# Long-convolution mixer and two feed-forward layers on one core: one unsplit block of eight instead of two, more splitting on POOL, and a 40-byte gap between POOL's operands

## The chip, the cores and the metric

The kernel runs on one core of a Trainium2 chip. The metric is the device time in microseconds of one execution; of several executions the median counts. Lower is better.

## What is computed

The reference, cut to its core (float32 throughout):

```
u = x * v                                    # x, v: 2 x 12480 x 128
h = (max(pos_emb @ w1, 0) @ w2) * exp(-0.01 * pos)
y = irfft(rfft(u, 2S) * rfft(h, 2S))[:S]     # long convolution along the sequence
a = x * y                                    # 24960 tokens x 128
h1 = a @ w_in1                               # 128 -> 2048
g1 = where(h1 > 0, h1, exp(min(h1, 0)) - 1)
b = g1 @ w_out1                              # 2048 -> 128
h2 = b @ w_in2
out = (h2 * cos(h2)) @ w_out2
```

## The kernel before

The work runs in three stages on one core, each engine with its own queue in program order. The order is written out by hand (`tc.manual_schedule()`), and the tile framework only adds the semaphores.

**Filter taps and convolution** (to about 690 us). The convolution is done as matrix products with DFT tables (`st_a` to `st_d`), and beside it the four weight matrices, which arrive as 64-bit floats, are decoded to float32, split in two and written to DRAM (`Decode`, from L109). POOL takes part with element-wise products, sums and differences.

**Layer 0 and layer 1** (from about 690 us to the end). Tokens stand in 52 tiles of T = 480 columns for each layer; the 2048 hidden features of a tile are done in NBLK = 8 blocks m of 256 (two halves e of 128). The loop at the end of the kernel (L641 to L656) goes through 2 x 52 x 8 = 832 blocks n. In iteration n it issues, in this order: `gemm1(n)`, at one block of the tile `split_x` for the next tile, in layer 1 `cosine(n - 1)`, the splits `split_g` of blocks one and two iterations old, and `gemm2(n - 5)` (LAG = 5).

A float32 product is done in one of two ways. **Split:** each factor is taken apart into a high part that TensorE reads in its reduced float32 (F32R) and a remainder, and three products are added: high x high, low weight x high, high weight x low. `gemm1` (L545) always does this: per block 2 halves x 3 = 6 matmuls of 480 columns. `gemm2` (L614) does it in blocks that are marked split: 6 matmuls. **Whole:** in a block marked `F.` in PLAN, `gemm2` multiplies unsplit float32 (tile `gf`, weights `wf`): one product per half, which stands as two matmul instructions in the trace, so four a block.

```
PLAN = ("AP PP F. AP PP F. PP PP".split(), "AP PP F. AP PP F. PP PP".split())
```

PLAN names for each layer and block who splits the activation g into `gh` and `gl` (`halves`, L102 to L107): the first letter is the engine of the rounding copy `gh` (A: ACT, L98, an ACTIVATE; P: POOL, L106, a TENSOR_SCALAR), the second that of the difference `gl = g - gh` (P: POOL, L107, a TENSOR_TENSOR of two inputs). Both are 128 x 960. A whole block gives POOL nothing to do. In layer 0 a block `PP` is split one iteration after its gemm1 and a block `AP` two after (`DELAY`, `DELAY_A`), the `PP` one first where both fall in one iteration; in layer 1 all are split two after. The state x of the next tile is split on POOL too (`xh`, `xl`, 128 x 480, `split_x` L525), issued at block 4 of a tile.

Activations: layer 0 takes Exp and Tanh on ACT (L556, L558) and two passes on DVE (L560, L562); layer 1 takes a rounding copy and Sin on ACT (L573, L582) and two passes on DVE (L575, L584). The activation g lies in the tile `e2` (shown as `e`), of which there are EB = 4 buffers; `gh` and `gl` have 5 each.

`skewed(pool, ...)` (L91) makes a tile 16 elements longer and starts the data `by` elements into it. SKEWS gives such starts for e2, gh and gl by layer and block, from 0 to 16 elements of 4 bytes:

```
SKEWS = (((0, 2, 0), (0, 10, 0), (0, 0, 0), (0, 4, 0), (0, 8, 0), (0, 0, 0), (0, 1, 0), (0, 10, 10)),
         ((2, 2, 0), (0, 0, 2), (0, 0, 0), (0, 6, 0), (0, 14, 0), (0, 0, 0), (2, 0, 2), (0, 16, 0)))
```

So in layer 0 `gh` of block 1 begins 40 bytes past a plain start while `e2` and `gl` begin at one; in layer 1 `e2` and `gh` of block 0 both begin 8 bytes past one. In the state split `x_in` and `xh` both begin at a plain start.

Weights are loaded whole for a layer: layer 0's on ACT's queue before its first block, layer 1's on SP's queue (`reload`) during the last tile of layer 0. A split block of output weights is 256 KB in two parts, a whole block 128 KB from `wf_d`, which `Decode.parts` writes in addition.

Of the kernel before, what the change touches and what calls it, by code (L numbers as in the profile page):

```python
# [9 lines left out]
F32 = mybir.dt.float32  # L10
F32R = mybir.dt.float32r
# [7 lines left out]
B, S, D, FO, DFF = 2, 12480, 128, 64, 2048  # L19
NA = 98  # L20
# [9 lines left out]
T = 480  # L30
NTC = B * S // T
NFT = DFF // 128
NBLK = NFT // 2
LAG = 5


PLAN = ("AP PP F. AP PP F. PP PP".split(), "AP PP F. AP PP F. PP PP".split())
FULL = [[m for m in range(NBLK) if p[m] == "F."] for p in PLAN]
XSPLIT = "PP"
EB = 4  # L40


SKEW = 10
SKEWS = (((0, 2, 0), (0, 10, 0), (0, 0, 0), (0, 4, 0), (0, 8, 0), (0, 0, 0), (0, 1, 0), (0, 10, 10)),
         ((2, 2, 0), (0, 0, 2), (0, 0, 0), (0, 6, 0), (0, 14, 0), (0, 0, 0), (2, 0, 2), (0, 16, 0)))

DELAY = (1, 2)
DELAY_A = (2, 2)
# [33 lines left out]
def hyena_moe_kernel(ctx: ExitStack, tc: tile.TileContext, x, v, pe, w1, w2,  # L82
# [8 lines left out]
    def skewed(pool, shape, dt, by, **kw):  # L91

        n = int(np.prod(shape[1:]))
        t = pool.tile([shape[0], n + 16], dt, **kw)[:, by:by + n]
        return t if len(shape) == 2 else t.rearrange("p (a b) -> p a b", a=shape[1])
# [6 lines left out]
    def halves(plan, hi, lo, full):  # L102
        if plan[0] == "A":
            copy_r(hi, full)
        else:
            ENG[plan[0]].tensor_scalar(hi, full, 1.0, 0.0, op0=ALU.mult, op1=ALU.add)  # L106
        ENG[plan[1]].tensor_tensor(lo, full, hi.bitcast(F32), op=ALU.subtract)  # L107
# [67 lines left out]
    with tc.manual_schedule():  # L175
        nc.vector.memset(below, BELOW)
        with ExitStack() as cs:
# [26 lines left out]
            with ExitStack() as fs:  # L204
                fp = fs.enter_context(tc.tile_pool(name="fp", bufs=4))
                f1 = fs.enter_context(tc.tile_pool(name="f1", bufs=1))
                f3 = fs.enter_context(tc.tile_pool(name="f3", bufs=3))
# [3 lines left out]
                NP = 4  # L211
# [13 lines left out]
                pes, rs, rr, hp_ = {}, {}, {}, {}  # L225
# [36 lines left out]

                def relu(c):
                    r = f3.tile([2 * FO, NP * NA], F32, name="r")
                    r_h = f3.tile([2 * FO, NP * NA], F32R, name="r_h")
                    r_l = f3.tile([2 * FO, NP * NA], F32R, name="r_l")
                    nc.scalar.activation(r, rs.pop(c), AF.Relu)
                    nc.gpsimd.tensor_scalar(r_h, r, 1.0, 0.0, op0=ALU.mult, op1=ALU.add)
                    nc.gpsimd.tensor_tensor(r_l, r, r_h.bitcast(F32), op=ALU.subtract)
                    rr[c] = (r_h, r_l)  # L270
# [40 lines left out]
            with ExitStack() as vs:  # L311
                p1 = vs.enter_context(tc.tile_pool(name="p1", bufs=1))
                p2 = vs.enter_context(tc.tile_pool(name="p2", bufs=2))
# [116 lines left out]
                    nc.sync.dma_start(xt_d[k, c * DC:(c + 1) * DC].rearrange("d a b -> a d b"), at)  # L430

                def alloc(name, dt):
                    return (p1 if name in ("sq", "keep", "power", "size") else p2).tile([128, 256], dt, name=name, tag=f"d_{name}")

                jobs = [(l, w, q) for l in range(2) for w in range(2) for q in range(DFF // 256)]
                ready = []
# [1 line left out]
                def bits_of_all():  # L438
                    nxt = Decode(alloc, 256, *jobs[0])
                    for i in range(len(jobs)):  # L440
                        dec = nxt
                        if i + 1 < len(jobs):
                            nxt = Decode(alloc, 256, *jobs[i + 1])
                        yield from dec.bits()
                        ready.append(dec)
# [33 lines left out]
        xp = ctx.enter_context(tc.tile_pool(name="xp", bufs=2))  # L479
        ep = ctx.enter_context(tc.tile_pool(name="ep", bufs=2))  # L480
        gp = ctx.enter_context(tc.tile_pool(name="gp", bufs=LAG))
# [37 lines left out]
        def load_x(j, q=nc.sync):  # L519
            if j < NTC:  # L520
                b, o = divmod(j * T, S)
                xin[j] = xp.tile([128, T], F32, name="x_in", tag="io")
                q.dma_start(xin[j], xt_d[b].rearrange("d a b -> d (a b)")[:, o:o + T])

        def split_x(l, j):  # L525
            src = xin.pop(j) if l == 0 else x1[:, j * T:(j + 1) * T]
            xh = xp.tile([128, T], F32R, name="xh")
            xl = xp.tile([128, T], F32R, name="xl")
            halves(XSPLIT, xh, xl, src)
            xsp[l, j] = (xh, xl)  # L530

        def g_tile(l, m, t):
            if m in FULL[l]:
                return skewed(gp, [128, 2, T], F32, 0, name="gf", tag="gh")
            return t

        def gemm1(n):
            l, j, m = blocks[n]
            xh, xl = xsp[l, j]

            def product(h, e):
                f = 2 * m + e
                wh, wl = layers[l].wt(0, 0, f), layers[l].wt(0, 1, f)
                for k, (a, b) in enumerate(((wh, xh), (wl, xh), (wh, xl))):
                    nc.tensor.matmul(h[:, 0:T], a, b, start=k == 0, stop=k == 2)  # L545

            if l == 0:
                hp, tp = hp_pool[0]
                u = skewed(ep, [128, 2, T], F32, SKEWS[l][m][0], name="e2", bufs=EB)
                gt = g_tile(l, m, u)  # L550
                hs, ts = [], []
                for e in range(2):
                    hs.append(hp.tile([128, 512], F32, name="h_ps"))
                    product(hs[e], e)
                for e in range(2):
                    nc.scalar.activation(u[:, e], hs[e][:, 0:T], AF.Exp)  # L556
                    ts.append(tp.tile([128, 512], F32, name="t_ps"))
                    nc.scalar.activation(ts[e][:, 0:T], hs[e][:, 0:T], AF.Tanh, scale=0.5)  # L558
                for e in range(2):
                    nc.vector.scalar_tensor_tensor(u[:, e], u[:, e], 1.0, ts[e][:, 0:T], op0=ALU.add, op1=ALU.mult)  # L560
                for e in range(2):
                    nc.vector.scalar_tensor_tensor(gt[:, e], u[:, e], 0.0, hs[e][:, 0:T], op0=ALU.min, op1=ALU.max)  # L562
                pend[n] = gt
            else:
                if 1 not in hp_pool:
                    ps0.close()
                    hp_pool[1] = ctx.enter_context(tc.tile_pool(name="hp2", bufs=3, space=PSUM))
                h = hp_pool[1].tile([128, 2, 512], F32, name="h_ps2")
                for e in range(2):
                    product(h[:, e], e)  # L570
                hv = h[:, :, 0:T]
                kq = ep.tile([128, 2, T], I32, name="e1")
                nc.scalar.activation(kq, hv, AF.Copy, scale=1.0 / TWO_PI, bias=0.25)  # L573
                rr = skewed(ep, [128, 2, T], F32, SKEWS[l][m][0], name="e2", bufs=EB)
                nc.vector.scalar_tensor_tensor(rr, kq, -TWO_PI, hv, op0=ALU.mult, op1=ALU.add)  # L575
                mid[n] = (rr, hv)

        def cosine(n):
            if n not in mid:
                return  # L580
            rr, hv = mid.pop(n)
            nc.scalar.activation(rr, rr, AF.Sin, bias=half_pi)  # L582
            gt = g_tile(*blocks[n][::2], rr)
            nc.vector.tensor_tensor(gt, rr, hv, op=ALU.mult)  # L584
            pend[n] = gt

        def split_g(n):
            if n not in pend:
                return
            gt = pend.pop(n)  # L590
            l, j, m = blocks[n]
            if m in FULL[l]:
                gg[n] = (gt, None)
                return
            gh = skewed(gp, [128, 2, T], F32R, SKEWS[l][m][1], name="gh")
            gl = skewed(gp, [128, 2, T], F32R, SKEWS[l][m][2], name="gl")
            halves(PLAN[l][m], gh, gl, gt)
            gg[n] = (gh, gl)

# [25 lines left out]
        def reload(n, wh):  # L625
            l, j, m = blocks[n]
            if l == 0 and j == NTC - 1:
                layers[1].load(nc.sync, wh, m)
# [8 lines left out]
        def delay(n):  # L637
            l, _, m = blocks[n]
            return (DELAY_A if PLAN[l][m][0] == "A" else DELAY)[l]

        for n in range(NBK + LAG):  # L641
            if n < NBK:
                l, j, m = blocks[n]
                gemm1(n)
                reload(n, 0)
                if m == NBLK // 2:
                    nl, nj = (l, j + 1) if j + 1 < NTC else (l + 1, 0)
                    if nl < 2:
                        split_x(nl, nj)
                    if l == 0:  # L650
                        load_x(j + 2)
            cosine(n - 1)
            for d in range(1, LAG):
                if 0 <= n - d < NBK and delay(n - d) == d:
                    split_g(n - d)
            if n >= LAG:  # L656
                gemm2(n - LAG)
                reload(n - LAG, 1)
# [38 lines left out]
```

## Time and profile before

| what | value |
|---|---|
| median of 3 runs | 2953.85 us (2953.04 to 2956.12) |
| the profiled execution | 2956.76 us, of it the span 2955.0 us |
| PE (matmul) busy | 2927.4 us, 99% of the span |
| DVE busy | 2507.0 us, 85% |
| POOL busy | 2426.0 us, 82% |
| ACT busy | 2074.1 us, 70% |
| mean granted TensorE clock | 0.994 of full speed |
| matmuls | 13268 |

The span runs from the first to the last instruction; the 1.76 us above it lie around it. Busy shares are means over the stages. Matmuls overlap and their ends are modelled, so PE's cost is better read from the distance between the starts of its groups in the timeline than from the busy time. A number in brackets behind an instruction of the timeline is the idle time of its engine just before it, and what ended it.

### The profile page before, as it was taken

What the parts mean: (1) busy time and instruction counts of PE and PEld (TensorE: products, weight loads), DVE (VectorE), ACT (ScalarE), POOL (GpSimd) and SP (SyncE); (2) the same over time, 40 slices, a digit from 0 to 9 for tenths busy, and PEclk for the clock granted to TensorE, in tenths of its full rate; (3) what the DMA queues carried; (4) which work ended last, traced back from release to release, by engine and by line L of the source; (5) the groups of instructions that cost most, each with busy time, mean ns of one, the idle gap of its engine ahead of it and who ended that gap; (6) DMA issues with size and microseconds to landing.
All of it is one profiled execution on the core that took longest, in us unless ns stands there. A gap on an engine that the chain in (4) does not pass through costs nothing.

```text
span 2955.0 us, 38859 instructions
## 1 busy us (share of the span) xinstructions
PE 2927.4 (99%) x13268; PEld 2340.5 (79%) x13268; DVE 2507.0 (85%) x3241; ACT 2074.1 (70%) x3228; POOL 2426.0 (82%) x1700
## 2 busy tenths in 40 slices
PE   8999999998999999999999999999999999999999
PEld 6878788786888887888888887887888888888887
DVE  5888888887888888888888888888888888888887
ACT  3323222324888888888888887888888888888887
POOL 5888888885888888888888887888888888888887
PEclk9999999998999999999999999999999999999999
DMA  3333333323000000000000001000000000000000
GB/s 104 89 84 92 89 95 90 86 75 93 11 11 14 11 14 11 14 11 11 14 11 14 11 11 54 11 14 10 14 11 11 14 11 14 11 14 11 12 13 14
DMA packets 82583, 96.19 MB, mean 33 GB/s; under 512 B 6107, under 2 KB 67577, under 8 KB 82387
## 3 DMA queue, kind: packets, MB, share of 16 engines
q1 hardware_dynamic: 76960, 88.07, 10.4%
q10 hardware_dynamic: 5426, 5.65, 0.6%
q8 instruction: 106, 1.74, 0.2%
q14 instruction: 91, 0.74, 0.1%
HBM read 59.16 MB, written 34.54 MB: 32 GB/s over the span
## 4 chain that ended last, share of the span: by engine, by line
PE 98%; DVE 1%; ACT 0%; issue 0%; POOL 0%; DMA 0%; POOLq 0%; ACTq 0%; DVEq 0%
PE o_ps L614 39%; PE h_ps L545 37%; PE ps_b L377 7%; PE ps_c L409 6%; PE ps_a L341 4%; PE ps_d L427 4%; PE h_ps L278 1%; PE w_ps L219 0%; PE r_ps L260 0%; DMA xt_d<-at 0%; ACT t_ps L558 0%; ACT e L556 0%; DVE e L562 0%; POOLq L693 0%; POOL u_t L322 0%
## 5 line engine op out<-in xcount | busy, mean ns | idle before, releaser
L107 POOL TENSOR_TENSOR gl<-e,gh 128x960 fp32r<-128x960 f32 x624 | 1272.8, 2047 | 147.7 <-ACT gh L98 113.0
L545 PE MATMUL h_ps<-xh,w 128*128 128x480 f32 x3328 | 1073.6, 403 | 10.4 <-DVE e L562 7.9
L545 PEld LDWEIGHTS h_ps<-xh,w 128*128 128x128 f32 x3328 | 627.6, 189 | 190.0 <-issue 85.5
L614 PE MATMUL o_ps<-gh,w 128*128 128x480 f32 x2496 | 748.1, 381 | 0.0
L575 DVE SCALAR_TENSOR_TENSOR e<-e,h_ps 128x960 f32<-128x960 int32 x416 | 480.2, 1154 | 199.7 <-ACT e L573 144.8
L560 DVE SCALAR_TENSOR_TENSOR e<-e,t_ps 128x480 f32<-128x480 f32 x832 | 542.8, 653 | 121.8 <-ACT t_ps L558 109.5
L545 PE MATMUL h_ps<-xl,w 128*128 128x480 f32 x1664 | 632.7, 380 | 0.1
L106 POOL TENSOR_SCALAR gh<-e 128x960 fp32r<-128x960 f32 x416 | 415.8, 1000 | 233.8 <-DVE e L562 174.1
L556 ACT ACTIVATE e<-h_ps 128x480 f32<-128x480 f32 x832 | 472.8, 568 | 186.5 <-PE h_ps L545 131.9
L573 ACT ACTIVATE e<-h_ps 128x960 int32<-128x960 f32 x416 | 404.5, 972 | 197.1 <-PE h_ps L545 194.1
L614 PEld LDWEIGHTS o_ps<-gh,w 128*128 128x128 f32 x2496 | 469.4, 188 | 76.0 <-issue 0.8
L614 PE MATMUL o_ps<-gl,w 128*128 128x480 f32 x1248 | 475.1, 381 | 1.9 <-POOL gl L107 1.9
L558 ACT ACTIVATE t_ps<-h_ps 128x480 f32<-128x480 f32 x832 | 475.8, 572 | 0.0
L582 ACT ACTIVATE e<-e,half_pi 128x960 f32<-128x960 f32 x416 | 453.4, 1090 | 0.3 <-DVE e L575 0.3
L562 DVE SCALAR_TENSOR_TENSOR e<-e,h_ps 128x480 f32<-128x480 f32 x624 | 377.9, 647 | 0.0
L614 PE MATMUL o_ps<-gf,wf 128*128 128x480 f32 x832 | 368.5, 565 | 0.0
L584 DVE TENSOR_TENSOR e<-e,h_ps 128x960 f32<-128x960 f32 x312 | 357.9, 1147 | 1.3 <-ACT e L582 1.2
L545 PEld LDWEIGHTS h_ps<-xl,w 128*128 128x128 f32 x1664 | 313.1, 188 | 50.9 <-POOL xl L107 0.8
L614 PEld LDWEIGHTS o_ps<-gl,w 128*128 128x128 f32 x1248 | 235.0, 188 | 40.1 <-POOL gl L107 2.7
L614 PEld LDWEIGHTS o_ps<-gf,wf 128*128 128x128 f32 x832 | 156.9, 189 | 100.8 <-issue 88.7
L98 ACT ACTIVATE gh<-e 128x960 fp32r<-128x960 f32 x208 | 208.2, 1001 | 11.0 <-PE o_ps L614 11.0
L377 PE MATMUL ps_b<-z_t,dft_t 128*128 128x360 f32 x512 | 165.7, 466 | 1.9 <-DVE y_t L393 1.7
(90 smaller groups left out, 3458.7 us busy)
## 6 DMA issues: line engine op xcount, KB each, us to landing
x_t<-in_x SPq DMA_DIRECT2D x32, 392.0 KB
v_t<-in_v SPq DMA_DIRECT2D x32, 392.0 KB
xt_d<-at SPq DMA_DIRECT2D x64, 196.0 KB
out<-ot SPq DMA_DIRECT2D x52, 240.0 KB
x_in<-xt_d SPq DMA_DIRECT2D x50, 240.0 KB
raw<-in_wi SPq DMA_DIRECT2D x16, 256.0 KB
w_d<-hi SPq DMA_DIRECT2D x32, 128.0 KB
w_d<-lo SPq DMA_DIRECT2D x32, 128.0 KB
```

Of the source, the lines that this page charges most:

```text
L106: ENG[plan[0]].tensor_scalar(hi, full, 1.0, 0.0, op0=ALU.mult, op1=ALU.add)
L107: ENG[plan[1]].tensor_tensor(lo, full, hi.bitcast(F32), op=ALU.subtract)
L377: nc.tensor.matmul(ps[:, r, 0:n], a[:, sl], b[:, q], start=j == 0 and i == 0, stop=j == 1 and i == len(mm) - 1)
L545: nc.tensor.matmul(h[:, 0:T], a, b, start=k == 0, stop=k == 2)
L556: nc.scalar.activation(u[:, e], hs[e][:, 0:T], AF.Exp)
L558: nc.scalar.activation(ts[e][:, 0:T], hs[e][:, 0:T], AF.Tanh, scale=0.5)
L560: nc.vector.scalar_tensor_tensor(u[:, e], u[:, e], 1.0, ts[e][:, 0:T], op0=ALU.add, op1=ALU.mult)
L562: nc.vector.scalar_tensor_tensor(gt[:, e], u[:, e], 0.0, hs[e][:, 0:T], op0=ALU.min, op1=ALU.max)
L573: nc.scalar.activation(kq, hv, AF.Copy, scale=1.0 / TWO_PI, bias=0.25)
L575: nc.vector.scalar_tensor_tensor(rr, kq, -TWO_PI, hv, op0=ALU.mult, op1=ALU.add)
L582: nc.scalar.activation(rr, rr, AF.Sin, bias=half_pi)
L614: nc.tensor.matmul(o, a, b[:, e], start=f == 0 and k == 0, stop=f == NFT - 1 and k == len(mm) - 1)
```

## The change

One block of eight (block 3) is whole in both layers, where blocks 2 and 5 were. The block that is now split in addition is split by POOL alone, so POOL makes five `PP` blocks a tile instead of four; two `AP` blocks remain (0 and 4, where 0 and 3 were). The starts of tiles that POOL reads together are set 40 bytes apart everywhere: SKEWS goes, `e2` and `gl` begin at a plain start and `gh` ten elements in; `xh`, the relu's `r_h` and, in the weight decoding, `lf` and `hi` get the same ten elements. In layer 1 the next tile's state is split at block 5 in place of 4; `load_x`, which stands in the same branch, is issued in layer 0 alone, where the block stays 4.

```diff
-PLAN = ("AP PP F. AP PP F. PP PP".split(), "AP PP F. AP PP F. PP PP".split())
+PLAN = ("AP PP PP F. AP PP PP PP".split(), "AP PP PP F. AP PP PP PP".split())
 FULL = [[m for m in range(NBLK) if p[m] == "F."] for p in PLAN]
 XSPLIT = "PP"
+
+XAT = (4, 5)
 EB = 4
 
-
 SKEW = 10
-SKEWS = (((0, 2, 0), (0, 10, 0), (0, 0, 0), (0, 4, 0), (0, 8, 0), (0, 0, 0), (0, 1, 0), (0, 10, 10)),
-         ((2, 2, 0), (0, 0, 2), (0, 0, 0), (0, 6, 0), (0, 14, 0), (0, 0, 0), (2, 0, 2), (0, 16, 0)))
...
-                    r_h = f3.tile([2 * FO, NP * NA], F32R, name="r_h")
+                    r_h = skewed(f3, [2 * FO, NP * NA], F32R, SKEW, name="r_h")
...
-                    return (p1 if name in ("sq", "keep", "power", "size") else p2).tile([128, 256], dt, name=name, tag=f"d_{name}")
+                    pool = p1 if name in ("sq", "keep", "power", "size") else p2
+                    if name in ("lf", "hi"):
+                        return skewed(pool, [128, 256], dt, SKEW, name=name, tag=f"d_{name}")
+                    return pool.tile([128, 256], dt, name=name, tag=f"d_{name}")
...
-            xh = xp.tile([128, T], F32R, name="xh")
+            xh = skewed(xp, [128, T], F32R, SKEW, name="xh")
...
-                u = skewed(ep, [128, 2, T], F32, SKEWS[l][m][0], name="e2", bufs=EB)
+                u = ep.tile([128, 2, T], F32, name="e2", bufs=EB)
...
-                rr = skewed(ep, [128, 2, T], F32, SKEWS[l][m][0], name="e2", bufs=EB)
+                rr = ep.tile([128, 2, T], F32, name="e2", bufs=EB)
...
-            gh = skewed(gp, [128, 2, T], F32R, SKEWS[l][m][1], name="gh")
-            gl = skewed(gp, [128, 2, T], F32R, SKEWS[l][m][2], name="gl")
+            gh = skewed(gp, [128, 2, T], F32R, SKEW, name="gh")
+            gl = gp.tile([128, 2, T], F32R, name="gl")
...
-                if m == NBLK // 2:
+                if m == XAT[l]:
```

## Rows read from the trace of the kernel before

**Rows 1.** The page: busy time of the engines; chain that ended last, by engine.

```profile
PE 2927.4 (99%) x13268; PEld 2340.5 (79%) x13268; DVE 2507.0 (85%) x3241; ACT 2074.1 (70%) x3228; POOL 2426.0 (82%) x1700
...
PE 98%; DVE 1%; ACT 0%; issue 0%; POOL 0%; DMA 0%; POOLq 0%; ACTq 0%; DVEq 0%
```

**Rows 2.** Windows (stretch: us, busy per engine, PEclk, DMA share, GB/s).

```profile
690.00:725.00 35.00, 26.84 (x86) 18.64 (x85) 20.99 (x37) 19.65 (x39) 17.36 (x13) 0.77 0.31 93
...
1000.00:1400.00 400.00, 400.00 (x1709) 321.00 (x1708) 356.50 (x595) 336.00 (x650) 329.11 (x224) 1.00 0.04 12
...
2300.00:2700.00 400.00, 400.00 (x1713) 321.62 (x1712) 330.03 (x299) 331.13 (x355) 338.29 (x224) 1.00 0.03 12
```

**Rows 3.** Timeline of PE, layer 1: start, us, what.

```profile
2203.93 0.60 PE L614 MATMUL o_ps<-gh,w 128*128 128x480 f32 x2
...
2206.56 0.60 PE L614 MATMUL o_ps<-gh,w 128*128 128x480 f32 x2
...
2209.15 1.77 PE L614 MATMUL o_ps<-gf,wf 128*128 128x480 f32 x4
2210.39 0.97 PE L545 MATMUL h_ps<-xh,w 128*128 128x480 f32 x2
...
2212.06 0.60 PE L614 MATMUL o_ps<-gh,w 128*128 128x480 f32 x2
...
2231.87 0.97 PE L545 MATMUL h_ps<-xh,w 128*128 128x480 f32 x2
```

**Rows 4.** Timeline of POOL, one tile of layer 0.

```profile
1016.70 1.00 POOL L106 TENSOR_SCALAR gh<-e 128x960 fp32r<-128x960 f32 x1 [1.38 <-DVE e L562]
1017.78 4.48 POOL L107 TENSOR_TENSOR gl<-e,gh 128x960 fp32r<-128x960 f32 x2
1022.20 1.01 POOL L106 TENSOR_SCALAR gh<-e 128x960 fp32r<-128x960 f32 x1
...
1025.16 1.00 POOL L106 TENSOR_SCALAR gh<-e 128x960 fp32r<-128x960 f32 x1
...
1030.12 0.99 POOL L106 TENSOR_SCALAR gh<-e 128x960 fp32r<-128x960 f32 x1 [1.99 <-DVE e L562]
1031.20 3.74 POOL L107 TENSOR_TENSOR gl<-e,gh 128x960 fp32r<-128x960 f32 x2
...
1038.24 0.99 POOL L106 TENSOR_SCALAR gh<-e 128x960 fp32r<-128x960 f32 x1 [1.43 <-DVE e L562]
```

**Rows 5.** Timeline of POOL, layer 1.

```profile
2220.47 2.28 POOL L107 TENSOR_TENSOR gl<-e,gh 128x960 fp32r<-128x960 f32 x1 [1.32 <-ACT gh L98]
2222.71 1.00 POOL L106 TENSOR_SCALAR gh<-e 128x960 fp32r<-128x960 f32 x1
2223.80 2.28 POOL L107 TENSOR_TENSOR gl<-e,gh 128x960 fp32r<-128x960 f32 x1
2226.04 0.59 POOL L106 TENSOR_SCALAR xh<-x 128x480 fp32r<-128x480 f32 x1
2226.72 1.24 POOL L107 TENSOR_TENSOR xl<-x,xh 128x480 fp32r<-128x480 f32 x1
2228.61 1.89 POOL L107 TENSOR_TENSOR gl<-e,gh 128x960 fp32r<-128x960 f32 x1 [0.65 <-ACT gh L98]
```

**Rows 6.** Groups by line and shape, 120 to 690 us (convolution): busy us, mean ns.

```profile
L322 POOL TENSOR_TENSOR u_t<-x_t,v_t 98x512 f32<-98x512 f32 x56 | 61.2, 1093 | 0.0
```

**Rows 7.** Timeline of all engines, last tile of layer 1.

```profile
2925.63 0.59 PE L545 MATMUL h_ps<-xh,w 128*128 128x480 f32 x2
...
2932.25 1.15 DVE L584 TENSOR_TENSOR gf<-e,h_ps 128x960 f32<-128x960 f32 x1
...
2943.97 1.00 POOL L106 TENSOR_SCALAR gh<-e 128x960 fp32r<-128x960 f32 x1 [0.89 <-DVE e L584]
...
2947.99 2.22 POOL L107 TENSOR_TENSOR gl<-e,gh 128x960 fp32r<-128x960 f32 x1
...
2950.26 0.49 PE L614 MATMUL o_ps<-gl,w 128*128 128x480 f32 x1 [1.60 <-POOL gl L107]
```

## The prediction

> **What bounds the kernel now.** I read the page first: PE is busy 99% of the span and 98% of the chain that ended last is PE's [rows 1]. Its busy time alone would not say that it is full, since the ends of matmuls are modelled; so I looked for gaps. In the windows PE is busy for all 400 us of a stretch of layer 0 and all 400 us of one of layer 1, at a full granted clock (1.00, the 2.4 GHz level), while DVE, ACT and POOL all leave idle time [rows 2]. So in both layers the end is set by what PE has to issue, and a change is worth what it takes off PE, as long as no other engine needs longer than a tile of PE.
>
> Next, what a block costs PE, from the starts of its groups [rows 3]. From one split block's gemm2 to the next (one gemm1 and one gemm2, 12 matmuls of reduced float32) takes 2206.56 - 2203.93 = 2.63 us, and 2.59 us to the next start, at 2209.15. That one is a whole block: its four matmuls delay the following gemm1 to 2210.39, the pass runs on into it, and the next gemm2 begins at 2212.06, 2.91 us after the whole one began. So a whole block is not the cheaper one, although it has four matmuls for six: it costs 0.3 us more. As a check, six blocks of 2.61 and two of 2.91 make 21.48 us, and the two tile starts shown lie 2231.87 - 2210.39 = 21.48 apart. (2209.15 is block 2's gemm2, which stands in the tile's last iteration, so a tile begins right after.) In layer 0 POOL's round takes 1038.24 - 1016.70 = 21.54 us [rows 4].
>
> **The change, part by part. PE:** each tile trades one whole block for one split one. With a tile at 21.53 us and the whole block at 2.91, the split one is (21.53 - 5.82) / 6 = 2.62, the difference 0.29 us; the rows themselves allow 0.28 to 0.32. Over 2 x 52 tiles that is 30.2 us saved (29 to 33). A tile then takes PE 21.24 us.
>
> **POOL** gets the work. Its round in layer 0 [rows 4]: the pair at 1016.70 is blocks 4 and 3 (PP first), then 6 at 1022.20 and 7 at 1025.16, then the pair 1 and 0 of the next tile at 1030.12, after which the state is split. A gl pass takes 4.48 / 2 = 2.24 us in blocks 4 and 3, whose gh starts 32 and 16 bytes past e, but 3.74 / 2 = 1.87 us in blocks 1 and 0 (40 and 8 bytes). In layer 1 it takes 2.28 us where e and gh start alike (blocks 0 and 1) [rows 5], and 2.22 us with 64 bytes between (block 7, in the last tile) [rows 7]. So what the gap of 40 bytes is worth is in the trace: block 1 of layer 0 has just the arrangement that all blocks get. I take 1.87 us for each gl. A PP split then costs 2.96 us from start to start (1022.20 to 1025.16), an AP split 1.87. The state: 0.68 us from xh to xl, and xl goes from 1.24 us [rows 5] to about 1.02, if a product of two inputs that are already 40 bytes apart, 1.093 us for 512 elements [rows 6], is scaled to 480; bounds 1.0 and 1.24.
>
> The sum for a tile: 5 x 2.96 + 2 x 1.87 + 0.68 + 1.02 = 20.24 us, against PE's 21.24. POOL fits, with 1.0 us to spare where layer 0 shows 1.38 + 1.99 = 3.37 us of idling now [rows 4]. It becomes the bound where the seven gl passes take over 1.87 + 1.0 / 7 = 2.01 us each.
>
> A page speaks against the new split here: the Trainium skill, GPSIMD Engine Reference, Performance versus the Vector engine, puts a two-input pass at about 2.6 cycles an element at 1.2 GHz, a floor of its read port; as an estimate from that page 960 elements take 2.08 us, seven passes 1.5 us more than in my sum, and POOL would set the tile at 21.7 us. The trace disagrees where the gap is 40 bytes (1.87 us) [rows 4].
>
> **Is POOL in time as well?** Follow layer 1, with times from a tile's first gemm1 (2210.39 in [rows 3]). Today block 3's gl starts at 2228.61 [rows 5], 18.22 in; the AP block there will be block 4, one iteration later: 20.84. Then gl 4, PP 5, 6 and 7 run without a pause to 20.84 + 1.87 + 3 x 2.96 = 31.6, which is 10.35 of the next tile. Block 0's gl, at 10.08 today, waits 0.3 us, and blocks 1 and 2 and the state follow to 10.35 + 1.87 + 5.92 + 1.70 = 19.84. There POOL idles until 20.84, so the queue closes on itself and doesn't grow. Who waits: the next tile's first product needs the state at 21.24 (it is split last before that, and the move by a block is why: at block 4 it would stand ahead of block 2's split), 1.4 us to spare. Block 7's gl, done at 31.6, is wanted by its gemm2 at 21.24 + 4 x 2.62 + 0.29 + 1.31 = 33.3, so 1.7 us early. In layer 0 the PP blocks go one iteration earlier, so they have 2.62 us more in hand than here; block 7, queued behind PP 5, gl 4 and PP 6, uses up 2.96 + 1.87 + 2.96 - 2 x 2.62 = 2.5 us of it. None of these reaches PE.
>
> **The rest, at nothing each.** The gaps in the relu, the weight decoding and the state make POOL's passes shorter in stages where PE sets the pace; a gain there is worth 0, a loss I can exclude by the same rows. The whole blocks' extra writes fall by 128 KB a layer on SP's queue; loads grow by 128 KB a layer, layer 0's on ACT's queue ahead of the first block: at the 93 GB/s of that stretch [rows 2] at most 1.4 us, if the last load is what the first gemm2 waits for. Layer 1's stand in SP's queue a tile ahead of their use. `load_x` is not moved.
>
> **The end.** In the last tile POOL is late already: PE waits 1.60 us for the last gl [rows 7]. Now block 5 is in that queue too, and POOL's 0.89 us of idling before block 6 goes. The three last splits take 3 x 2.96 and finish no sooner than today; between 0 and +2 us, I take +1.
>
> **Sum:** -30.2 + 1.0 = -29.2 us. The profiled execution took 2956.8 us (span 2955.0 and 1.8 around it), so 2927.6. The median of the runs lies 2.9 us below the profiled one, so about 2925 for a median.
>
> **The rivals.** (a) *POOL sets the end*, the case on the slower side. The shorter pass belongs to today's placements of buffers and doesn't carry over: e2 and gl become 64 bytes shorter. Then gl costs 2.28 us; PP, as block 1 of layer 1 shows, 2226.04 - 2222.71 = 3.33 us, and the tile 5 x 3.33 + 2 x 2.24 + 0.68 + 1.24 = 23.05 us, 1.5 more than now: 2954 + 104 x 1.52 = 3112. It decides from 2.01 us a pass on. Against it: with four buffers of e and five of gh in turn, the passes shown keep to their 1.87 or 2.24 by gap alone. Chance 0.04.
>
> (a') *POOL's pass has a floor somewhere between*, above the 2.01 us at which it decides and below the 2.24 us of the next rows up. At their middle, 2.12, the tile is 20.24 + 7 x 0.25 = 21.99 us and the time 2954 + 104 x 0.46 = 3002. Against it: the passes of [rows 4, 5] with 8, 24 or 40 bytes between e and gh stand at 1.87 to 1.89. Chance 0.02. The skill's page named above would put the pass at 2.08 us and so the time at about 2973, an estimate from that page.
>
> (b) *A second chain, of ACT and DVE, is just as full in layer 1*, and part of the gain is lost. h has three buffers there, so gemm1 of block n + 3 waits for block n's second DVE pass. That pass ended 2933.40 for a gemm1 begun at 2925.63, 7.77 us [rows 7], and three split iterations last 7.86. Today each such slow block (those whose ACT queue carries an AP copy) has a whole gemm2 within those three iterations; block 2 will not, as the whole block's gemm2 moves to iteration 0. If ACT is 0.1 to 0.3 us later, PE waits that long once a tile: 52 x 0.1 to 0.3 = 5 to 15 us back, 2930 to 2940. A late state split would look alike. Chance 0.12.
>
> (c) *No net effect*, 2954: whole and split blocks cost the same in place, or waits eat all of 0.29 us. [Rows 3] speak against it. Chance 0.03.
>
> **How the numbers follow.** The forecast, PE's tile shorter by 0.28 to 0.32 us in both layers, has 0.79: 2925, and with its bounds (29 to 33 us saved, 0 to 2 at the end, up to 1.4 at the loads) 2920 to 2928. Runs of before spread over 3 us, so 2918 to 2931 for it. To hold 8 in 10 with the sizes' own errors I take in (b)'s nearer part, up to 2937. A measurement can tell about 0.2%, 5.9 us: all of the forecast and all of (b) lie beyond that, (a) and (a') are slower and (c) within, apart from a little of (b) that could come out worse.
>
> **What would show it.** Right: starts of two split gemm2 still 2.62 us apart, one 2.91 in a tile, tile starts 21.24 apart; all gl at 1.87 to 1.9, xl near 1.02; POOL busy about 95% of both layers with one pause of some 1 us a tile, before gl of block 4 or PP 5; PE at 100% in the windows. Wrong: gl at 2.2 or more (a); PE gaps of 0.1 to 0.3 us once a tile, released by DVE L584 at block 5's gemm1 (b) or by POOL xl at a tile's start; a split block's 2.62 us grown.

## The result and the profile after

The changed kernel takes 2927.34 us (median of 4 runs, 2926.68 to 2929.37) against 2953.44 for the kernel before: a ratio of 0.991, 95% interval 0.9898 to 0.9923, or 26.1 us less. The forecast was 2925, with 2918 to 2937. The profiled execution took 2926.68 us, of it the span 2924.9.

First the same lines of the page and the windows as in [rows 1, 2].

```profile
PE 2895.9 (99%) x13476; PEld 2377.2 (81%) x13476; DVE 2502.7 (86%) x3241; ACT 2060.4 (70%) x3228; POOL 2587.7 (88%) x1908
...
PE 97%; POOL 1%; DMA 1%; ACT 1%; DVE 1%; issue 0%; ACTq 0%; POOLq 0%; DVEq 0%
```

```profile
1000.00:1400.00 400.00, 400.00 (x1770) 333.09 (x1769) 360.21 (x604) 339.02 (x661) 368.63 (x265) 1.00 0.05 13
...
2300.00:2700.00 400.00, 400.00 (x1770) 332.29 (x1769) 333.89 (x302) 333.39 (x359) 369.12 (x265) 1.00 0.03 12
```

208 matmuls more and yet less time: PE is busy in all 400 us of both stretches, as it was, but more tiles go through them. POOL stands at 368.6 and 369.1 of 400 us, where it had 329.1 and 338.3.

The timeline of PE in layer 1 answers to [rows 3]:

```profile
2206.84 0.59 PE L616 MATMUL o_ps<-gh,w 128*128 128x480 f32 x2
...
2208.15 0.60 PE L547 MATMUL h_ps<-xh,w 128*128 128x480 f32 x2
...
2209.46 1.77 PE L616 MATMUL o_ps<-gf,wf 128*128 128x480 f32 x4
2210.70 0.98 PE L547 MATMUL h_ps<-xh,w 128*128 128x480 f32 x2
...
2212.39 0.60 PE L616 MATMUL o_ps<-gh,w 128*128 128x480 f32 x2
...
2215.01 0.60 PE L616 MATMUL o_ps<-gh,w 128*128 128x480 f32 x2
...
2230.70 1.77 PE L616 MATMUL o_ps<-gf,wf 128*128 128x480 f32 x4
```

A split block still takes 2209.46 - 2206.84 = 2.62 us (and 2215.01 - 2212.39 = 2.62 after the whole one), the whole one 2212.39 - 2209.46 = 2.93, and there is one whole block from tile to tile, 2230.70 - 2209.46 = 21.24 us apart. The six matmuls of a split gemm2 hold PE for 2208.15 - 2206.84 = 1.31 us, 0.22 each. A gemm1 takes another 1.31, so the four of the whole block cost 2.93 - 1.31 = 1.62 us, 0.40 each.

POOL's timeline of one tile of layer 1, from one pause to the next, answers to [rows 5]:

```profile
2207.41 1.88 POOL L106 TENSOR_TENSOR gl<-e,gh 128x960 fp32r<-128x960 f32 x1 [1.05 <-ACT gh L97]
2209.26 0.99 POOL L105 TENSOR_SCALAR gh<-e 128x960 fp32r<-128x960 f32 x1
2210.33 1.88 POOL L106 TENSOR_TENSOR gl<-e,gh 128x960 fp32r<-128x960 f32 x1
2212.18 1.00 POOL L105 TENSOR_SCALAR gh<-e 128x960 fp32r<-128x960 f32 x1
...
2216.20 3.90 POOL L106 TENSOR_TENSOR gl<-e,gh 128x960 fp32r<-128x960 f32 x2
...
2225.92 0.59 POOL L105 TENSOR_SCALAR xh<-x 128x480 fp32r<-128x480 f32 x1
2226.60 1.04 POOL L106 TENSOR_TENSOR xl<-x,xh 128x480 fp32r<-128x480 f32 x1
2228.66 1.89 POOL L106 TENSOR_TENSOR gl<-e,gh 128x960 fp32r<-128x960 f32 x1 [1.02 <-ACT gh L97]
```

Every gl takes 1.88 to 1.89 us, xl 1.04, and the queue has its one marked pause of 1.0 us where the forecast put it, ahead of block 4's gl. There is a new wait, in these lines of the waits in 2300 to 2700 us:

```profile
DVE e L577 <- POOL gh L105: 27.5, 56, 0.7
...
POOL gl L106 <- ACT gh L97: 19.6, 19, 1.1
```

DVE's first pass now waits for a slot of e that POOL frees, up to 0.7 us at a time, without PE waiting for DVE in that stretch.

In the table below "tile" is the mean distance between the starts of successive xh on POOL, without the first and last three, in layer 0 and layer 1.

| kernel | median us | tile, layer 0 | tile, layer 1 |
|---|---|---|---|
| before | 2953.4 | 21.53 | 21.50 |
| changed | 2927.3 | 21.25 | 21.26 |
| no gap at gh | 3076.4 | 22.68 | 22.73 |
| two whole blocks, with the gap | 2956.7 | 21.56 | 21.57 |
| state split at block 4 | 2927.8 | 21.25 | 21.26 |
| POOL one copy more | 2926.7 | 21.25 | 21.26 |
| POOL three copies more | 2995.4 | 21.94 | 21.96 |
| gap at gh alone | 2927.4 | 21.24 | 21.25 |
| no whole block | 2922.2 | 20.95 | 21.42 |
| none in layer 0, one in layer 1 | 2916.0 | 20.95 | 21.28 |
| none, DVE in halves in layer 1 | 2976.2 | 20.95 | 22.48 |

The medians were taken in four sets, with the kernel before at 2953.0 to 2954.1 us in them.

### The profile page after: what moved, and what is told of

The parts are those of the page before. It is cut to its first block, busy times and chain, and to the rows that moved or that the text cites. A ratio compares the mean times of both kernels' runs of the same rounds, so it can differ in the third digit from the quotient of the medians.

```text
span 2924.9 us, 39791 instructions
## 1 busy us (share of the span) xinstructions
PE 2895.9 (99%) x13476; PEld 2377.2 (81%) x13476; DVE 2502.7 (86%) x3241; ACT 2060.4 (70%) x3228; POOL 2587.7 (88%) x1908
## 4 chain that ended last, share of the span: by engine, by line
PE 97%; POOL 1%; DMA 1%; ACT 1%; DVE 1%; issue 0%; ACTq 0%; POOLq 0%; DVEq 0%
PE o_ps L616 38%; PE h_ps L547 37%; PE ps_b L376 7%; PE ps_c L408 6%; PE ps_a L340 4%; PE ps_d L426 4%; PE h_ps L277 1%; PE w_ps L218 0%; PE r_ps L259 0%; DMA w<-w_d 0%; DMA xt_d<-at 0%; POOL z_t L348 0%; ACT e L558 0%; ACT t_ps L560 0%; DVE e L562 0%
## 5 line engine op out<-in xcount | busy, mean ns | idle before, releaser
L106 POOL TENSOR_TENSOR gl<-e,gh 128x960 fp32r<-128x960 f32 x728 | 1369.6, 1887 | 109.8 <-ACT gh L97 61.4
L616 PE MATMUL o_ps<-gh,w 128*128 128x480 f32 x2912 | 870.6, 380 | 0.0
L616 PEld LDWEIGHTS o_ps<-gh,w 128*128 128x128 f32 x2912 | 547.7, 188 | 87.6 <-POOL gh L105 0.4
L105 POOL TENSOR_SCALAR gh<-e 128x960 fp32r<-128x960 f32 x520 | 518.0, 996 | 68.5 <-DVE e L564 62.0
L616 PE MATMUL o_ps<-gl,w 128*128 128x480 f32 x1456 | 554.4, 381 | 3.2 <-POOL gl L106 3.2
L564 DVE SCALAR_TENSOR_TENSOR e<-e,h_ps 128x480 f32<-128x480 f32 x728 | 440.6, 646 | 0.0
L586 DVE TENSOR_TENSOR e<-e,h_ps 128x960 f32<-128x960 f32 x364 | 417.4, 1147 | 1.3 <-ACT e L584 1.2
L616 PEld LDWEIGHTS o_ps<-gl,w 128*128 128x128 f32 x1456 | 274.1, 188 | 47.8 <-POOL gl L106 4.4
L616 PE MATMUL o_ps<-gf,wf 128*128 128x480 f32 x416 | 184.3, 566 | 0.0
L348 POOL TENSOR_TENSOR z_t<-za,zb 128x720 f32<-128x720 f32 x96 | 141.0, 1468 | 26.1 <-DVE zb L345 26.1
```

The lines of the kernel that those rows point to most:

```text
L616: nc.tensor.matmul(o, a, b[:, e], start=f == 0 and k == 0, stop=f == NFT - 1 and k == len(mm) - 1)
```

## Experiments: is it PE's 0.3 us, and what lets POOL carry its part?

My theory was that the gain is PE's alone, 0.29 us a tile for each whole block that becomes a split one, as long as POOL's work fits into PE's tile, and that the 40 bytes are what makes it fit. The first rival was that the gain is POOL's shorter passes; the second that the gap is beside the point.

**Two whole blocks, with the gap**

```diff
-PLAN = ("AP PP PP F. AP PP PP PP".split(), "AP PP PP F. AP PP PP PP".split())
+PLAN = ("AP PP F. AP PP F. PP PP".split(), "AP PP F. AP PP F. PP PP".split())
```

> The changed kernel with the old list of blocks (two whole, four PP, two AP), so the gap of 40 bytes and the later state split alone. Theory (the gain is PE's 0.29 us a tile and nothing else): tile 21.53 us, time 2953 us as before, POOL idling more than 4 us a tile with gl at 1.88. Rival (the gain comes from POOL's shorter passes): 2927 us.

Measured: 2956.68 us, a ratio to before of 1.0012 (1.0003 to 1.0021). Every gl stood at 1.88 to 1.90 us, and POOL was busy 311.6 and 312.2 us of 400, with more idling; nothing was gained. The gap alone buys no time; the rival falls. It even cost some 3 us, which the part on why the prediction was right takes up.

**No gap at gh**

```diff
-            gh = skewed(gp, [128, 2, T], F32R, SKEW, name="gh")
+            gh = skewed(gp, [128, 2, T], F32R, 0, name="gh")
```

> The changed kernel, but gh begins at a plain start like e and gl, so the 40 bytes are gone in the block splits alone. Theory (PE sets the pace as long as POOL fits, and the gap makes it fit): every gl pass takes 2.28 us, POOL's tile 5 x 3.33 + 2 x 2.24 + 1.70 = 22.83 us against PE's 21.24, POOL without a pause, and the time 2927 + 104 x 1.59 = 3092 us. Rival (the gap is beside the point, PE sets the pace anyway): 2927 us.

Measured: 3076.35 us, a ratio of 1.0417 (1.0396 to 1.0438). The windows, and the waits of 2300 to 2700 us:

```profile
1000.00:1400.00 400.00, 387.63 (x1656) 305.74 (x1655) 334.85 (x566) 315.75 (x619) 391.24 (x248) 1.00 0.04 12
2300.00:2700.00 400.00, 386.21 (x1657) 307.55 (x1656) 310.98 (x283) 313.04 (x335) 391.16 (x248) 1.00 0.03 11
```

```profile
DVE e L577 <- POOL gl L106: 68.7, 70, 1.1
PEld h_ps L547 <- PE o_ps L616: 33.2, 52, 0.9
...
PE h_ps L547 <- DVE e L586: 12.3, 34, 0.5
```

POOL is full, PE no longer is, and the chain is readable: DVE waits for gl to free e, PE waits for DVE to free h. The tile is POOL's, 22.7 us; the rows of before had summed to 22.83, and 3092 us. Without the 40 bytes the additional split would have cost 4% instead of gaining 1%.

**How much POOL has in hand.** A spare copy of the state, once or three times a tile:

```diff
             halves(XSPLIT, xh, xl, src)
+            idle = xp.tile([128, T], F32R, name="idle")
+            for _ in range(1):
+                nc.gpsimd.tensor_scalar(idle, src, 1.0, 0.0, op0=ALU.mult, op1=ALU.add)
```

> The changed kernel with one more rounding copy of the state on POOL in every tile, written to a spare tile that nothing reads: 0.6 us more for POOL. Theory (POOL has 1.0 us in hand, the pauses of 1.02 to 1.08 us a tile in its timeline): the pause shrinks to about 0.45 us, tile 21.25 us and time 2927 us unchanged, within 3. Rival (POOL is already a bound, PE's full busy time hiding it): 2927 + 104 x 0.6 = 2990 us.

> The same with three such copies, 1.7 to 1.8 us more for POOL. Theory: POOL passes PE at 1.0 us, so the tile grows by 0.65 to 0.8 us, no pause on POOL is left, 2995 to 3010 us. Rival (there is more in hand than the pause shows, since buffers absorb it): 2927 to 2950 us.

Measured: 2926.67 us with one (ratio 0.991, 0.9893 to 0.9926), 2995.36 with three. With one, the pauses fell to about half a microsecond and the time stayed:

```profile
POOL gh L105 <- DVE e L567: 8.9, 19, 0.5
```

(waits, 1000 to 1400 us; the changed kernel has 19.9 us in 19 such pauses there). With three the tile grew by 0.69 to 0.70 us, and POOL's timeline in layer 1 shows what they took:

```profile
2210.23 1.95 POOL L534 TENSOR_SCALAR idle<-x 128x480 fp32r<-128x480 f32 x3
2212.14 1.89 POOL L106 TENSOR_TENSOR gl<-e,gh 128x960 fp32r<-128x960 f32 x1
```

That is 2212.14 - 2210.23 = 1.91 us; less the 0.70 that showed, 1.2 us was in hand, a little more than the 1.0 of my sum: beside its pause of 1.02 us the changed kernel's round holds another 0.16 us, inside the pair at 2216.20 (3.90 us, where the run with three copies has 3.74 for the pair). So POOL's limit is measured from both sides.

**What of the rest was needed.** The state split at block 4 in layer 1:

```diff
-XAT = (4, 5)
+XAT = (4, 4)
```

> The changed kernel with layer 1's state split issued at block 4 again, ahead of block 2's split in POOL's queue. Theory (PE sets the pace, and block 2's gl, 1.7 us later at about 19.8 us of the tile, is still before its gemm2 at 19.95 to 20.4): 2927 us, at most 5 more. Rival (the move by a block is needed): block 2's gl is late, which delays gemm2 or the slot of e by 0.5 to 1 us once a tile in layer 1, 2953 to 2980 us.

Measured: 2927.78 us (ratio 0.9916, 0.99 to 0.9933), tiles the same to 0.01 us. The move by a block neither helps nor harms; the prediction gave it as a reason why POOL is in time, and that was more than it is. The gap at gh alone, the other four tiles at a plain start:

```diff
-            xh = skewed(xp, [128, T], F32R, SKEW, name="xh")
+            xh = xp.tile([128, T], F32R, name="xh")
...
-                    if name in ("lf", "hi"):
+                    if False:
...
-                    r_h = skewed(f3, [2 * FO, NP * NA], F32R, SKEW, name="r_h")
+                    r_h = f3.tile([2 * FO, NP * NA], F32R, name="r_h")
```

> The changed kernel with the gap kept for gh alone: the state's xh, the relu's r_h and the decoder's lf and hi begin at a plain start. Theory 1 (the other gaps buy nothing, since PE sets the pace where they stand): xl takes 1.23 us, POOL's tile 20.45 us, still under PE's, 2927 us. Theory 2 (they cost a little: in the run with two whole blocks matmuls of the state's parts follow one another by 218.4 to 219.1 ns where before shows 217.7, some 45 ns a tile, and only the state's tiles moved there): spacing back at 217.7, tile 21.21 us, 2922 to 2924 us. Rival (the gap is needed everywhere): over 2933 us.

Measured: 2927.41 us (ratio 0.9909, 0.9895 to 0.9924). Theory 1 holds: xl at 1.23 us, no gain lost. Theory 2 falls: the mean spacing of the state's matmuls went back to 217.2 to 218.1 ns, but that of gh and gl, which were not touched, rose from 217.6 and 218.2 to 218.7 and 219.2 in layer 0, and the tile shrank by only 0.01 us.

**Following PE's price further.** If a whole block costs PE 0.3 us more than a split one, the last one should go as well. POOL has no room for it, so ACT makes gh and DVE gl:

```diff
-PLAN = ("AP PP PP F. AP PP PP PP".split(), "AP PP PP F. AP PP PP PP".split())
+PLAN = ("AP PP PP AD AP PP PP PP".split(), "AP PP PP AD AP PP PP PP".split())
```

> The changed kernel with the last whole block of each tile split too, gh by ACT and gl by DVE (AD in place of F.), so POOL has nothing more to do, ACT 1.0 us a tile more, DVE some 1.2 us more. Theory (PE sets the pace and a whole block costs it 0.28 to 0.29 us more than a split one): tile 20.95 us, 2927 - 104 x 0.29 = 2897 us. Rival 1 (ACT's and DVE's chain in layer 1 has only some 0.1 to 0.3 us in hand): PE waits for DVE once a tile by about 1 us in layer 1, and the gain is lost there: 2912 to 2965 us. Rival 2: the DVE pass reads both inputs from the memory that POOL reads, and the two exclude one another for 1.2 us a tile: POOL 20.24 + 1.2 = 21.44 us a tile, 2948 us. The Trainium skill, SBUF - State Buffer, SBUF: two separate sides, states such an exclusion for a DVE operation with two SBUF inputs against a GpSimd one; no run so far shows it.

Measured: 2922.2 us (ratio 0.9895, 0.9881 to 0.991). Layer 0 did what the theory says, 20.95 us a tile; layer 1 got slower, 21.42 us, as rival 1 says. One such place, from the timeline of all engines in layer 1:

```profile
2216.23 1.24 DVE L106 TENSOR_TENSOR gl<-e,gh 128x960 fp32r<-128x960 f32 x1
...
2216.54 1.81 POOL L106 TENSOR_TENSOR xl<-x,xh 128x480 fp32r<-128x480 f32 x1
...
2217.39 1.14 DVE L577 SCALAR_TENSOR_TENSOR e<-e,h_ps 128x960 f32<-128x960 int32 x1
...
2218.45 1.14 DVE L586 TENSOR_TENSOR e<-e,h_ps 128x960 f32<-128x960 f32 x1
...
2219.08 0.38 PE L616 MATMUL o_ps<-gl,w 128*128 128x480 f32 x1
...
2219.74 0.67 PE L547 MATMUL h_ps<-xh,w 128*128 128x480 f32 x2 [0.28 <-DVE e L586]
```

The DVE pass pushes both passes behind it, and the gemm1 three blocks on waits for the second: the chain of rival (b), seen in its place. The 0.28 us of idling understates the loss, since the ends of matmuls are modelled: from start to start it is 2219.74 - 2219.08 = 0.66 us where matmuls here follow one another by 0.22, so 0.44 us, nearly all of the 0.47 by which this tile is longer than layer 0's. The second line shows rival 2's mechanism too: xl takes 1.81 us beside the DVE pass and 1.04 in the changed kernel. This bears out what the Trainium skill (SBUF — State Buffer, SBUF: two separate sides) states of a DVE operation with two SBUF inputs against a GpSimd one. In layer 0 the pass held up is a rounding copy, 1.78 us for 1.00. Either way POOL's round is 0.8 us longer, but POOL kept up: layer 0 holds PE's 20.95.

So one layer alone:

```diff
-PLAN = ("AP PP PP F. AP PP PP PP".split(), "AP PP PP F. AP PP PP PP".split())
+PLAN = ("AP PP PP AD AP PP PP PP".split(), "AP PP PP F. AP PP PP PP".split())
```

> The last whole block split by ACT and DVE in layer 0 alone; layer 1 keeps its one. Theory (the run without any whole block gained 0.30 us a tile in layer 0, 20.95 us, and lost 0.16 us in layer 1 to PE's waits for DVE): 2927 - 52 x 0.30 = 2912 us, layer 1 at 21.26 us. Rival (what layer 1 lost there came over from layer 0, as POOL and DVE enter it late): layer 1 over 21.3 us, 2916 to 2922 us.

Measured: 2915.98 us (2914.37 to 2918.06), a ratio to before of 0.9872 (0.9857 to 0.9887): the fastest of all, 38 us under before and 11 under the changed kernel. Layer 1 is at 21.28 us, 0.02 above the changed kernel's, so the theory holds for the tiles, though the time stands at the edge of the rival's range; of the 15.6 us expected 11.4 came. Of the other 4 the traces place about 3: the 0.02 us make 1 us over layer 1, and at the change of layers three tiles (the last of layer 0 and the first two of layer 1, from gemm1 to gemm1) took 68.8 us against 67.3, where 0.3 less was due, so 1.9. There PE waited 2.66 us, and TensorE's granted clock was 0.89 from 1785 to 1800 us; in the changed kernel it waited 2.30 us, and the clock was 1.00 from 1800 to 1815. Whether the new plan or chance brought the lower clock no run separates.

A last attempt put DVE's part in layer 1 into two halves, an iteration apart, to fit its idle time:

```diff
+            if (l, PLAN[l][m]) == (1, "AD"):
+                copy_r(gh, gt)
+                rest_of[n] = (gh, gl, gt)
+                half(n, 0)
+            else:
+                halves(PLAN[l][m], gh, gl, gt)
...
+            nc.vector.tensor_tensor(gl[:, e], gt[:, e], gh[:, e].bitcast(F32), op=ALU.subtract)
...
+            if n - 3 in rest_of:
+                half(n - 3, 1)
+                del rest_of[n - 3]
```

> No whole block in either layer, as in the run with none, but in layer 1 the DVE part of block 3 is issued as two passes of 480 columns, one iteration apart, in place of one of 960. Theory (in layer 1 PE waited because one DVE pass of 1.2 us put the passes behind it 0.7 us late, more than the 0.1 to 0.3 us that the chain through h's three buffers has in hand; a half, 0.63 us, goes into DVE's idle time of 0.4 to 0.5 us an iteration and leaves 0.2): layer 1 at 20.95 to 21.05 us a tile, 2916 - 52 x (0.2 to 0.3) = 2900 to 2905 us. Rival 1 (any DVE pass there makes PE wait): layer 1 at 21.3 us or more, 2916 us or more. Rival 2 (POOL, lengthened by 0.8 us where the DVE pass runs beside it, becomes the bound at 21.05 to 21.15 us a tile): POOL without a pause, 2906 to 2912 us.

Measured: 2976.15 us (ratio 1.0082, 1.0068 to 1.0095), layer 1 at 22.48 us a tile. It is on rival 1's side, but neither of its size nor for its reason; the timeline of all engines has that:

```profile
2302.37 1.88 POOL L106 TENSOR_TENSOR gl<-e,gh 128x960 fp32r<-128x960 f32 x1 [0.86 <-ACT gh L97]
2302.65 2.11 DVE L611 TENSOR_TENSOR gl<-e,gh 128x480 fp32r<-128x480 f32 x1
...
2304.22 1.40 POOL L105 TENSOR_SCALAR gh<-e 128x960 fp32r<-128x960 f32 x1
...
2304.69 1.14 DVE L577 SCALAR_TENSOR_TENSOR e<-e,h_ps 128x960 f32<-128x960 int32 x1
...
2307.04 0.67 PE L547 MATMUL h_ps<-xh,w 128*128 128x480 f32 x2 [1.26 <-DVE e L586]
```

The second half came 0.28 us after a gl had begun on POOL and took 2.11 us instead of 0.70 (the first half, in the same tile): it ended at 2304.76, 0.51 us after POOL's pass, so nearly all of it ran once that pass was over, and POOL's next pass took 1.40 us instead of 1.00. So it goes in nearly every tile: 49 of the 52 second halves took over 2 us. The line's own summary (duration in ns, least, median and most) mixes first and second halves:

```profile
L611 DVE TENSOR_TENSOR gl<-e,gh x104: 652/1406/2125, 1805.4 to 2954.6; 128x480 fp32r<-128x480 f32 x104
```

In the run with the undivided pass DVE came first and POOL paid; here POOL came first and DVE paid, and DVE's delay is the one that PE waits for, 1.26 us of idling a tile.

## Why the prediction was right

**PE's term.** Foreseen: 0.29 us a tile, 30.2 us in all, from a split block at 2.62 and a whole one at 2.91. The changed kernel's starts show 2.62 and 2.93. The tiles shrank by 0.28 us in layer 0 and 0.24 in layer 1, which over 52 tiles each makes 27.2 us: 3 us less than the term, below its bounds of 29 to 33. The term was too large at both of its ends: the tile after the change, worked out as 21.24 us, came out as 21.25 and 21.26, and the tile before it, taken as 21.53 in both layers, is 21.50 in layer 1. Put against a kernel of the same layout the price is larger: the run with two whole blocks and the gap has 21.56 and 21.57, so a whole block costs 0.31 us more than a split one, and going from one to none in layer 0 gave 0.30. What else the change brings, then, costs PE 0.03 to 0.06 us a tile, by that run against the kernel before: the tiles' new places in memory, POOL's shorter passes and, in layer 1, the later state split. The split's block alone moved nothing (21.25 and 21.26 at either block). PE's matmuls follow one another 1 ns or so later in some operand groups, and the groups that do so were others in the run with the gap at gh alone, where the state's xh has none; that the places in memory decide it is likely but not shown. The prediction had put all this at nothing for PE, without a row for it.

**POOL's sum.** Foreseen: 20.24 us a tile, 1.0 us to spare, gl at 1.87, xl at 1.02. Measured: gl 1.88 to 1.89, xl 1.03 to 1.04, pauses of 1.0 to 1.1 us, and 1.2 us in hand by the run with three copies. One sign was read off wrongly: POOL was to be busy 95% of both layers and is at 92% in the windows, since the sum goes from start to start and so takes in the 0.1 us or less between a rounding copy and the next pass, which the windows do not count. The decision to take the passes with 40 bytes between their operands as the price of all seven was the one that carried the forecast, and the run without the gap shows what the other price would have done. The Trainium skill's figure (GPSIMD Engine Reference, Performance versus the Vector engine), by which the pass would take 2.08 us as an estimate, is not borne out for operands 40 bytes apart (1.88 us); it lies between these and unspaced passes (2.21 to 2.31 us).

**In time.** No PE wait appears in the windows of either layer, as worked out; PE does wait at the change of layers (2.30 and 0.78 us after, 1.8 and 0.5 before), which the prediction left out. The chain of rival (b) did not decide: block 5's gemm1 never waits in the stretches looked at. That it was nearly full is shown by the run without whole blocks, where 1.2 us more on DVE cost PE 0.44 us a tile.

**The end.** Foreseen: +1 us, between 0 and 2. In the last tile PE now waits for gl three times, where [rows 7] show 1.60 us for the last one:

```profile
2913.85 0.48 PE L616 MATMUL o_ps<-gl,w 128*128 128x480 f32 x1 [0.62 <-POOL gl L106]
...
2916.77 0.48 PE L616 MATMUL o_ps<-gl,w 128*128 128x480 f32 x1 [1.27 <-POOL gl L106]
...
2919.70 0.48 PE L616 MATMUL o_ps<-gl,w 128*128 128x480 f32 x1 [1.26 <-POOL gl L106]
```

From the last gemm1's start, 2938.97 before and 2907.09 after, to the end of the span it is 16.0 us before and 17.8 after: +1.8. With it, -27.2 + 1.8 = -25.4 us, against the 26.1 less that the medians show. The two profiled executions differ by more, 30.1 us. Part of that is the start of layer 0, which varies from run to run: from its first gemm1 to the next tile's, layer 0's first tile took 25.8 us before and 23.0 after, with a granted clock of 0.77 [rows 2] and 0.81 from 690 to 725 us, and 20.7 in the run with one copy more, at 0.90.

**The rest at nothing.** The weight decoding's passes on POOL fell from 0.73 to 0.64 us each. Layer 0's first gemm1 began at 693.9 us where it had begun at 695.0 (695.2 in the run with the gap at gh alone), so the first stages gave 1 us at most; PE was busy 612.3 of the 615 us from 75 to 690 in all three. The move of the state split is worth nothing either way.

## What to carry to other kernels

Price an instruction that seems cheaper by the distance between the starts of its neighbours: four unsplit float32 matmuls held PE longer than six reduced ones. When work is moved to an engine that then runs close to full, sum its whole round from rows, look for the same operation at several placements in the trace before believing one duration, and measure what is in hand by adding spare work. Work given to DVE and POOL on the same memory should be checked for exclusion from both sides, since who pays depends on who comes first.

## What the runs showed of the hardware

- A POOL pass of two inputs, 128 x 960, took 1.88 to 1.89 us with the operands 40 bytes apart and 2.21 to 2.31 us with both at a plain start, in the same kernel otherwise. Of the nine gaps between e and gh in the kernel before, 4, 8, 24, 40 and 56 bytes had medians of 1.89 us, and 0, 16, 32 and 64 bytes 2.24 to 2.28: not every gap helps, and of these nine the slow ones are the multiples of 16 bytes. By length, 480 and 960 elements took 1.04 and 1.89 us spaced, 1.23 and 2.28 unspaced: 1.8 against 2.2 ns an element.
- A DVE pass with two inputs in SBUF and a POOL pass did not run side by side: xl on POOL took 1.81 us for 1.04, a rounding copy 1.78 for 1.00, the DVE half 2.11 us for 0.70. DVE's passes with one input in PSUM kept 1.15 us beside POOL at 92% of the time.
- A matmul instruction of 480 columns held PE for 0.40 us in unsplit float32 and for 0.22 in reduced float32: 1.62 us for the four of a whole block against 1.31 for the six of a split one.
- The same matmuls in the same order took PE 0.03 to 0.06 us a tile more when tiles' places in memory and, with them, the times of POOL's passes had changed; this was not explained.
